# Second-half attention tiles: the minimum on GpSimd in integers, whole float32 probabilities, and the product with v on two column halves

## The chip, the core and the metric

The kernel runs on one core of a Trainium2 chip. Its five engines have queues of their own and meet by semaphores: TensorE (PE in the rows, with its weight loads as PEld), VectorE (DVE), ScalarE (ACT), GpSimd (POOL) and SyncE (SP, which issues DMAs). The metric is the device time of one execution in microseconds; lower is better.

## The reference, cut to what matters

Attention with a top-32 mask comes first, then a mixture of experts, then a gated MLP over all 2304 tokens (4 batches of 576 tokens, 8 heads of 64).

```python
scores = scale * np.matmul(q, k.transpose(0, 1, 3, 2))                  # 576 x 576 for each head
kth = np.partition(scores, -top_k, axis=-1)[..., -top_k:-top_k + 1]     # top_k = 32
attn = exp(where(scores >= kth, scores, -1e9) - max);  attn /= attn.sum(-1) + 1e-9
x = np.matmul(attn, v)                                                  # then reshaped to 2304 x 512
...                                                                     # routed experts, each row to one of 8
out = (silu(x @ w_gate) * (x @ w_val)) @ w_out                          # gated MLP, 512 -> 1536 -> 512
```

## The kernel before

Work is cut by pairs of heads: 16 pairs (4 batches with 4 each), and 9 tiles of 128 rows in a pair, 144 tiles in all. The first 9 pairs (81 tiles) are called `whole` in the code; they run alone, and the other 7 pairs (63 tiles) run while the experts and the gated MLP of the first two batches are woven between them. The page calls none of this by name, so the text calls them the first stage (13 to 336 us of the profile) and the second stage (336 to 812 us). After 858 us no attention is left: the experts and the MLP of the other two batches follow.

A tile goes through these steps. `head` makes the scores of 128 rows against 576 keys on TensorE (L226, bank `pS`) and ScalarE copies them to `sc` (L236). `rows_tile` finds the 32nd largest score of each row on VectorE: it takes the larger of the two halves of a row elementwise (L247, 288 wide) and the smaller (L265, or the pair L262 and L263), then runs the 8-at-a-time maximum and its replacement (L252, L267, L268), and the last maximum reads both halves, 576 wide. In the first stage the smaller half comes from GpSimd with the scores read as 32-bit integers: sum of both halves (`sm`, L262), minus the larger (L263); and the mask is made on TensorE (L277) and ScalarE (L278). In the second stage the smaller half is a VectorE minimum (L265), and VectorE also makes the masked probabilities `pp` from `sc`, the 32nd value and the exponentials `e` (L281).

`late` takes the probabilities on. In the first stage (`trans_whole`, `pv_whole`) `pp` is transposed as it is, in float32, 5 transposes for a tile (L321), copied to `pt` (L323), and multiplied with v, 5 float32 products of 64 columns (L331), then transposed back (L337). In the second stage GpSimd first splits `pp` into a high and a low part `pr` in the one-pass type float32r (L285 to L287), TensorE makes 9 transposes (L295) and 9 products with v, which is split as well (`vv`, L183 and L184; products L305), and a product with `fold` adds the two halves of 64 partitions (L312). A pair makes four products with v: two of 256 rows and two of 320. `prep` loads and transposes q and k of a pair; their copies into `nat` are made by GpSimd in the first stage and by ScalarE in the second (L163), and by ScalarE for the very first pair, which borrows the two `pr` buffers so that two of its four steps need not wait for the single `nat`.

The order on each engine comes from a scheduler at build time. It follows the order in which the code is written (one string for each stage says when transposes and products of earlier tiles come), with its own estimate of costs; the experts and the MLP are issued between tiles in proportion to the tiles that are done.

Of the kernel before, what the change touches and what calls it, by code (L numbers as in the profile page):

```python
# [32 lines left out]
class Kernel:  # L33
# [78 lines left out]

    def prep(self, R, b, h, whole):
        """Loads a pair of heads and puts what its tiles need into R; yields between steps."""
# [3 lines left out]

        def tile_of(nm):
            return (sb.tile([P, 2, 5, D], F32, name="vv", bufs=3) if nm == "v" and whole else  # L120
                    sb.tile([P, 2, 5, D], F32, name="raw", bufs=2))

        def load(nm, t, i, parts=(0, 1)):
# [19 lines left out]
        raws = {nm: tile_of(nm) for nm in ("k", "q")}  # L143
# [6 lines left out]
        for i in range(2):  # L150
            for nm, w in (("k", 2), ("q", 3)):
# [3 lines left out]
                if first and (i == 0) == (nm == "q"):  # L155
                    t = sb.tile([P, 2 * S], F32R, name="pr", bufs=2)[:, :15 * D].rearrange("p (c e) -> p c e", c=5)
                else:
                    t = sb.tile([P, 5, 3 * D], F32R, name="nat", bufs=1)
                o = t[:, :n, :w * D].rearrange("p c (t e) -> p c t e", t=w)
                src = raws[nm][:, i, :n, :]  # L160
                if first or (not whole):
                    for z in range(0, w, 2):
                        nc.scalar.activation(o[:, :, z, :], src, AF.Copy)  # L163
                elif w == 3:
                    nc.gpsimd.tensor_scalar(o[:, :, 0:3:2, :], src[:, :, None, :].to_broadcast([P, n, 2, D]),
                                            1.0, 1.0, op0=OP.mult, op1=OP.mult)
                else:
                    nc.gpsimd.tensor_scalar(o[:, :, 0, :], src, 1.0, 1.0, op0=OP.mult, op1=OP.mult)
# [70 lines left out]
    def rows_tile(self, R, i, c, Z, on_pe, sc):  # L239
        nc, ps, S = self.nc, self.ps, self.S  # L240
        sb, X = (self.at1, 1) if on_pe else (self.at, 0)
        W = S // 2
        scf = sc.rearrange("p a b -> p (a b)")
        rest = sb.tile([P, 2, W], F32, name="rest", bufs=3 if X else 2)
        hj, lo = rest[:, 0], rest[:, 1]
        hi = sb.tile([P, W], F32, name="hi", bufs=3) if X else hj
# [8 lines left out]
        pp = sb.tile([P, S], F32, name="pp", bufs=3 if X else 2)  # L255
# [15 lines left out]
        if on_pe:  # L271
            u = sb.tile([P, 2, W], F32R, name="e", bufs=3)
            nc.scalar.activation(u, sc, AF.Relu, bias=kth, scale=-1.0)
            pS = self.ps1.tile([P, 2, 512], F32, name="pM", bufs=1)
            self.scores(R, i, c, pS, stop=False)
            for x in range(2):
                nc.tensor.matmul(pS[:, x, :W], self.nidr, u[:, x, :], start=False, stop=True)  # L277
            nc.scalar.activation(pp.rearrange("p (a b) -> p a b", a=2), pS[:, :, :W], AF.Exp, bias=nb, scale=0.125,  # L278
                                 accum_out=Z)
        else:  # L280
            nc.vector.scalar_tensor_tensor(pp, scf, kth, e, op0=OP.is_ge, op1=OP.mult, accum_out=Z)  # L281
        if on_pe:
# [7 lines left out]
    def trans(self, pr, dests):  # L290
        nc = self.nc
        for a, z in ((0, 4), (4, 8), (8, 9)):
            p = self.pt_bank(F32R)
            for c in range(a, z):
                self.anchor = nc.tensor.transpose(p[:, c - a, :], pr[:, c * P:(c + 1) * P], self.idr)  # L295
            pf = p.bitcast(F32)
            for (T, do, so, n) in dests:
                nc.scalar.activation(T[:, a:z, do:do + n], pf[:, :z - a, so:so + n], AF.Copy)  # L298

    def pv(self, R, i, T, W, outs):  # L300
        nc, sb, D = self.nc, self.at, self.D
        vv = R["v"][i]
# [13 lines left out]
    def trans_whole(self, pp, dests):  # L316
        nc = self.nc
        for a, z, k in ((0, 4, P), (4, 5, 64)):
            p = self.pt_bank()
            for c in range(a, z):  # L320
                nc.tensor.transpose(p[:k, c - a, :], pp[:, c * P:c * P + k], self.idn)  # L321
            for (T, do, so, n) in dests:
                nc.scalar.activation(T[:k, a:z, do:do + n], p[:k, :z - a, so:so + n], AF.Copy)  # L323

    def pv_whole(self, R, i, T, W, outs):
        nc, sb, D = self.nc, self.at, self.D
        v = R["v"]
        po = self.pt_bank().rearrange("p a b -> p (a b)")
        for n in range(5):
            k = P if n < 4 else 64  # L330
            nc.tensor.matmul(po[:D, :W], v[:k, i, n, :], T[:k, n, :W], start=(n == 0), stop=(n == 4))  # L331
        oT = sb.tile([P, 320], F32, name="oT", bufs=1)[:D]
        nc.scalar.activation(oT[:, :W], po[:D, :W], AF.Copy)
        yield
        p = self.pt_bank()
        for j, (so, n, dst) in enumerate(outs):
            nc.tensor.transpose(p[:n, j, :D], oT[:, so:so + n], self.idn[:D, :D])  # L337
        for j, (so, n, dst) in enumerate(outs):
            nc.scalar.activation(dst, p[:n, j, :D], AF.Copy)

# [925 lines left out]
```

## Time and profile before

| what | value |
|---|---|
| median of 3 runs | 1313.6 us (1313.06 to 1316.07) |
| the profiled execution: span from first to last instruction | 1314.5 us |
| VectorE, TensorE, GpSimd busy in the first stage (323 us) | 315.2, 311.5, 223.5 us |
| the same in the second stage (476 us) | 445.5, 436.4, 321.5 us |
| the same from 858 us on (456 us) | 264.1, 434.5, 171.0 us |

The profiled execution's span is 0.9 us above the median of the runs, so one may stand for the other. Busy time is the time covered by an engine's records. Records of TensorE overlap: each one lasts from a matmul's start to its end, and the next starts before that end, so its busy time is more than the time that the work needs.

### The profile page before, as it was taken

What the parts mean: (1) busy time and instruction counts of PE and PEld (TensorE: products, weight loads), DVE (VectorE), ACT (ScalarE), POOL (GpSimd) and SP (SyncE); (2) the same over time, 40 slices, a digit from 0 to 9 for tenths busy, and PEclk for the clock granted to TensorE, in tenths of its full rate; (3) what the DMA queues carried; (4) which work ended last, traced back from release to release, by engine and by line L of the source; (5) the groups of instructions that cost most, each with busy time, mean ns of one, the idle gap of its engine ahead of it and who ended that gap; (6) DMA issues with size and microseconds to landing.
All of it is one profiled execution on the core that took longest, in us unless ns stands there. A gap on an engine that the chain in (4) does not pass through costs nothing.

```text
span 1314.5 us, 22493 instructions
## 1 busy us (share of the span) xinstructions
PE 1229.2 (94%) x7499; PEld 1076.6 (82%) x7500; DVE 1043.6 (79%) x2390; ACT 790.7 (60%) x1734; POOL 740.5 (56%) x888
## 2 busy tenths in 40 slices
PE   6899999999998998998998999899999999999995
PEld 5677777777787887887987789889998789898994
DVE  7999999999988889899999998217888638275570
ACT  5888887888855565665655545317677634343440
POOL 6866765766466676876787656413131335555550
PEclk9999999999998999997989999999999999999998
DMA  6411110101177787864556675469888644453520
GB/s 186 172 55 38 38 38 20 34 25 28 38 253 270 251 285 245 292 220 150 181 185 236 233 269 188 163 216 348 282 295 271 206 167 128 125 170 122 153 80 27
DMA packets 128577, 219.68 MB, mean 167 GB/s; under 512 B 20420, under 2 KB 86980, under 8 KB 122180
## 3 DMA queue, kind: packets, MB, share of 16 engines
q1 hardware_dynamic: 121428, 179.37, 41.6%
q0 software_dynamic: 7024, 38.78, 9.2%
q8 instruction: 62, 1.02, 0.3%
q14 instruction: 63, 0.52, 0.1%
HBM read 178.28 MB, written 41.95 MB: 168 GB/s over the span
## 4 chain that ended last, share of the span: by engine, by line
PE 36%; DVE 16%; DMA 5%; issue 3%; ACT 2%; POOL 2%; SPq 0%; DVEq 0%; ACTq 0%; POOLq 0%
PE m L1191 6%; PE m L1193 6%; PE m L1192 6%; PE m L1214 3%; PE m L1215 3%; PE m L1216 3%; DVE pp L281 3%; DVE tops L268 3%; DMA wraw<-in_moe_w_dram 2%; DVE rest L267 2%; DVE rest L247 2%; DVE rest L265 1%; DVE whl L664 1%; PE m L1124 1%; PE pT L295 1%
## 5 line engine op out<-in xcount | busy, mean ns | idle before, releaser
L268 DVE MAX8 tops<-rest 128x8 f32<-128x288 f32 (+1 forms) x432 | 227.2, 544 | 1.6
L1191 PE MATMUL m<-x2h,whl 128*128 128x384 f32 x576 | 198.0, 345 | 8.4 <-DVE th L1200 3.5
L1192 PE MATMUL m<-x2l,whl 128*128 128x384 f32 x576 | 196.7, 342 | 0.0
L1193 PE MATMUL m<-x2h,whl 128*128 128x384 f32 x576 | 196.4, 342 | 0.0
L1160 POOL TENSOR_TENSOR whl<-wfly,whl 128x1024 fp32r<-128x1024 f32 x54 | 129.8, 2404 | 109.0 <-ACT whl L1159 108.9
L267 DVE MATCH_REPLACE8 rest<-tops,rest 128x288 f32<-128x288 f32 x351 | 152.9, 437 | 0.0
L1159 ACT ACTIVATE whl<-wfly 128x1024 fp32r<-128x1024 f32 x69 | 73.2, 1061 | 97.9 <-PE m L1193 58.3
L236 ACT ACTIVATE sc<-pS 128x576 f32<-128x576 f32 x144 | 93.9, 652 | 54.5 <-DVE pp L281 38.6
L226 PE MATMUL pS<-kT,qT 128*128 128x288 f32 x512 | 108.8, 329 | 14.5 <-ACT sc L236 12.7
L1191 PEld LDWEIGHTS m<-x2h,whl 128*128 128x128 f32 x576 | 109.8, 191 | 10.7 <-DVE th L1200 4.4
L1192 PEld LDWEIGHTS m<-x2l,whl 128*128 128x128 f32 x576 | 110.2, 191 | 0.4
L1193 PEld LDWEIGHTS m<-x2h,whl 128*128 128x128 f32 x576 | 110.0, 191 | 0.5
L298 ACT ACTIVATE pt<-pT 128x512 fp32r<-128x512 f32 (+3 forms) x210 | 87.0, 464 | 35.1 <-PE pT L295 33.6
L1203 DVE TENSOR_TENSOR h2l<-th,h2h 128x384 fp32r<-128x384 f32 x36 | 85.9, 2386 | 21.5 <-ACT h2h L1202 21.5
L331 PE MATMUL pT<-pt,vv 128*64 128x256 f32 (+3 forms) x360 | 102.0, 415 | 0.8 <-ACT pt L323 0.8
L996 DVE TENSOR_TENSOR whl<-wraw,whl 128x1024 fp32r<-128x1024 f32 x64 | 80.2, 1266 | 27.7 <-ACT whl L995 23.6
L262 POOL TENSOR_TENSOR sm<-sc 128x288 int32<-128x288 int32 x81 | 73.5, 908 | 45.9 <-ACT sc L236 44.4
L226 PEld LDWEIGHTS pS<-kT,qT 128*128 128x128 f32 x512 | 79.5, 199 | 19.6 <-ACT sc L236 16.2
L1200 DVE SCALAR_TENSOR_TENSOR th<-th,m 128x384 f32<-128x384 f32 x72 | 39.0, 541 | 67.0 <-ACT th L1199 67.0
L995 ACT ACTIVATE whl<-wraw 128x1024 fp32r<-128x1024 f32 x64 | 67.5, 1060 | 38.0 <-DMA wraw<-in_moe_w_dram 23.3
L1214 PE MATMUL m<-whl,h2h 128*128 128x512 f32 x216 | 86.5, 404 | 2.4 <-ACT whl L642 1.7
L1215 PE MATMUL m<-whl,h2h 128*128 128x512 f32 x216 | 86.0, 398 | 0.0
(236 smaller groups left out, 3354.6 us busy)
## 6 DMA issues: line engine op xcount, KB each, us to landing
wfly<-w2s SPq DMA_DIRECT2D x69, 512.0 KB
whl<-in_moe_w_dram SPq DMA_DIRECT2D x32, 1024.0 KB
wraw<-in_moe_w_dram SPq DMA_DIRECT2D x64, 512.0 KB
whl<-w2s POOLq DMA_DIRECT2D x31, 1024.0 KB, 5.6
w2s<-h2h SPq DMA_DIRECT2D x8, 1024.0 KB
w2s<-whl SPq DMA_DIRECT2D x8, 1024.0 KB
io<-xa SPq DMA_DIRECT2D x18, 256.0 KB
out_dram<-io SPq DMA_DIRECT2D x18, 256.0 KB
```

Source lines behind the costliest of these rows:

```text
L226: m = self.nc.tensor.matmul(pS[:, x, :W], l, r[:, x * W:(x + 1) * W], start=(n == 0), stop=stop and n == len(ops) - 1)
L236: self.nc.scalar.activation(sc, pS[:, :, :W], AF.Copy, scale=BIG)
L267: nc.vector.match_replace(hj, h[:, (j - 1) * 8:j * 8], hi if j == 1 else hj, NEG)
L268: nc.vector.max(h[:, j * 8:(j + 1) * 8], hj if j < 3 else rest.rearrange("p a b -> p (a b)"))
L298: nc.scalar.activation(T[:, a:z, do:do + n], pf[:, :z - a, so:so + n], AF.Copy)
L331: nc.tensor.matmul(po[:D, :W], v[:k, i, n, :], T[:k, n, :W], start=(n == 0), stop=(n == 4))
L1160: self.fly_engine.tensor_tensor(lo, raw, hi.bitcast(F32), op=OP.subtract)
L1191: nc.tensor.matmul(pz, wh[:, z, k, :], xh[:, k, :], start=(k == 0), stop=False)
L1192: nc.tensor.matmul(pz, wh[:, z, k, :], xl[:, k, :], start=False, stop=False)
L1193: nc.tensor.matmul(pz, wl[:, z, k, :], xh[:, k, :], start=False, stop=(k == 3))
L1214: nc.tensor.matmul(po[t], hh[:, f, s], wh[:, k, :], start=(f == 0), stop=False)
L1215: nc.tensor.matmul(po[t], hh[:, f, s], wl[:, k, :], start=False, stop=False)
```

## The change

For the 63 tiles of the second stage: the smaller half is made by GpSimd in integers, as in the first stage; `pp` is not split, it is transposed in float32; v is not split; the copies of q and k into `nat` move from ScalarE to GpSimd. For all 144 tiles: the five products with v write the two halves of the 128 PSUM partitions in turn (products 0, 2, 4 to the lower 64, products 1 and 3 to the upper), and the product with `fold` adds them, where the first stage had a transpose back. The first pair no longer borrows `pr` buffers, which are gone: all four of its steps use the single `nat`. Buffers `hi`, `rest` and `pp` are three deep in both stages. All the rest (comments, an own tile `xt` for a copy that used `pp`) is the same work.

```diff
 prep:
-                if first and (i == 0) == (nm == "q"):
-                    t = sb.tile([P, 2 * S], F32R, name="pr", bufs=2)[:, :15 * D].rearrange("p (c e) -> p c e", c=5)
-                else:
-                    t = sb.tile([P, 5, 3 * D], F32R, name="nat", bufs=1)
+                t = sb.tile([P, 5, 3 * D], F32R, name="nat", bufs=1)
...
-                if first or (not whole):
+                if first:
                     for z in range(0, w, 2):
                         nc.scalar.activation(o[:, :, z, :], src, AF.Copy)
...
-        R["v"] = vv = []
-        for i in range(2):
-            t = sb.tile([P, 5, 2 * D], F32R, name="vv", bufs=3)
-            nc.gpsimd.tensor_scalar(t[:, :, :D], raw[:, i], 1.0, 1.0, op0=OP.mult, op1=OP.mult)
-            nc.gpsimd.tensor_tensor(t[:, :, D:], raw[:, i], t[:, :, :D].bitcast(F32), op=OP.subtract)
-            vv.append(t)
-            yield
 rows_tile:
-        if X:
-            sm = sb.tile([P, W], I32, name="sm", bufs=2)
-            sci = sc.bitcast(I32)
-            nc.gpsimd.tensor_tensor(sm, sci[:, 0, :], sci[:, 1, :], op=OP.add)
-            nc.gpsimd.tensor_tensor(lo.bitcast(I32), sm, hi.bitcast(I32), op=OP.subtract)
-        else:
-            nc.vector.tensor_tensor(lo, sc[:, 0, :], sc[:, 1, :], op=OP.min)
+        sm = sb.tile([P, W], I32, name="sm", bufs=2)
+        sci = sc.bitcast(I32)
+        nc.gpsimd.tensor_tensor(sm, sci[:, 0, :], sci[:, 1, :], op=OP.add)
+        nc.gpsimd.tensor_tensor(lo.bitcast(I32), sm, hi.bitcast(I32), op=OP.subtract)
...
-        pr = sb.tile([P, 2 * S], F32R, name="pr", bufs=2)
-        nc.gpsimd.tensor_scalar(pr[:, :S], pp, 1.0, 1.0, op0=OP.mult, op1=OP.mult)
-        nc.gpsimd.tensor_tensor(pr[:, S:S + 64], pp[:, 512:], pr[:, 512:S].bitcast(F32), op=OP.subtract)
-        nc.gpsimd.tensor_tensor(pr[:, S + 64:], pp[:, :512], pr[:, :512].bitcast(F32), op=OP.subtract)
-        return pr
 trans:
-        for a, z in ((0, 4), (4, 8), (8, 9)):
-            p = self.pt_bank(F32R)
+        for a, z, k in ((0, 4, P), (4, 5, 64)):
+            p = self.pt_bank()
             for c in range(a, z):
-                self.anchor = nc.tensor.transpose(p[:, c - a, :], pr[:, c * P:(c + 1) * P], self.idr)
+                self.anchor = nc.tensor.transpose(p[:k, c - a, :], pp[:, c * P:c * P + k], self.idn)
 pv:
-        for n in range(9):
-            self.anchor = nc.tensor.matmul(po[:, :W], vv[:, n if n < 5 else n - 5, :], T[:, n, :W], start=(n == 0),
-                                           stop=(n == 8))
+        for n in range(5):
+            k = P if n < 4 else 64
+            self.anchor = nc.tensor.matmul(po[(n % 2) * D:(n % 2 + 1) * D, :W], v[:k, i, n, :], T[:k, n, :W],
+                                           start=(n < 2), stop=(n >= 3))
...
-    def trans_whole(self, pp, dests):
-    def pv_whole(self, R, i, T, W, outs):
```

How the order on the engines moves is shown at three places of the second stage. On VectorE, behind the row update of the third expert: `sc` are the scores, `rest` and `hi` the halves, `tops` the list of maxima, `pp` the masked probabilities. Before:

```order
L247 TENSOR_TENSOR rest<-sc 128x288
L265 TENSOR_TENSOR rest<-sc 128x288
L252 MAX tops_67<-rest 128x8
L267 MATCH_REPLACE rest<-tops_67,rest 128x288
L281 SCALAR_TENSOR_TENSOR pp,z<-sc,tops_67,e 128x576
L268 MAX tops_67<-rest 128x8
L267 MATCH_REPLACE rest<-tops_67,rest 128x288
L268 MAX tops_67<-rest 128x8
```

The same place after the change (L230 is the old L247, L235 the old L252, L247 and L248 the old L267 and L268, L252 the old L281):

```order
L230 TENSOR_TENSOR hi<-sc 128x288
L235 MAX tops_67<-hi 128x8
L247 MATCH_REPLACE rest<-tops_67,hi 128x288
L248 MAX tops_67<-rest 128x8
L252 SCALAR_TENSOR_TENSOR pp,z<-sc,tops_67,e 128x576
L247 MATCH_REPLACE rest<-tops_67,rest 128x288
L248 MAX tops_67<-rest 128x8
```

The minimum between the maximum of halves and the first list is gone; nothing else of a tile leaves the engine. On GpSimd, around the scatter of the second expert's rows to DRAM (`xa<-io`) and the next gather (`io<-xa`), before:

```order
L1012 DMA xa_203<-io,ids_5335 1153x512
L285 TENSOR_SCALAR pr<-pp 128x576
L286 TENSOR_TENSOR pr<-pp,pr 128x64
L287 TENSOR_TENSOR pr<-pp,pr 128x512
L643 TENSOR_TENSOR h2h<-h2h 128x1024
L1005 DMA io<-xa_203,ids_5335 128x512
```

The same place after the change:

```order
L960 DMA xa_201<-io,ids_5307 1153x512
L244 TENSOR_TENSOR sm<-sc 128x288
L417 TENSOR_TENSOR x<-x,rt 64x64
L237 TENSOR_SCALAR nb<-tops_67 128x1
L245 TENSOR_TENSOR rest<-sm,hi 128x288
L244 TENSOR_TENSOR sm<-sc 128x288
L245 TENSOR_TENSOR rest<-sm,hi 128x288
L237 TENSOR_SCALAR nb<-tops_67 128x1
L953 DMA io<-xa_201,ids_5307 128x512
```

The three splits of `pp` are replaced by the integer pair, which now stands behind the scatter and ahead of the gather. On TensorE, around a product with v of 320 rows (`pt` and `vv`), before:

```order
L305 MATMUL pT<-pt,vv 128x320 x8
L295 MATMUL pT<-idr,pr 128x128 x4
L305 MATMUL pT<-pt,vv 128x320
L295 MATMUL pT<-idr,pr 128x128 x4
L1106 MATMUL m<-idn,th 128x128 x4
L226 MATMUL pS<-kT,qT 128x288 x4
L295 MATMUL pT<-idr,pr 128x128
L312 MATMUL pT<-fold,oT 128x64 x2
```

The same place after the change:

```order
L280 MATMUL pT<-pt,vv 64x320 x5
L269 MATMUL pT<-idn,pp 128x128 x4
L269 MATMUL pT<-idn,pp 64x128
L209 MATMUL pS<-kT,qT 128x288 x4
L1054 MATMUL m<-idn,th 128x128 x4
L287 MATMUL pT<-fold,oT 128x64 x2
```

Nine one-pass products become five float32 products of 64 columns, and nine transposes become five; the scores and the experts' work keep their places among them.

## Rows read from the trace of the kernel before

**Rows 1.** Stages: busy us (instructions) of PE, PEld, DVE, ACT, POOL; clock, DMA share, GB/s.

```profile
13.00:336.00 323.00, 311.51 (x2007) 240.12 (x2008) 315.21 (x968) 271.88 (x709) 223.47 (x353) 0.98 0.20 61
336.00:812.00 476.00, 436.41 (x2784) 393.42 (x2785) 445.52 (x1071) 279.36 (x667) 321.48 (x396) 0.95 0.67 224
858.00:1314.00 456.00, 434.47 (x2435) 399.72 (x2433) 264.07 (x302) 215.19 (x299) 170.95 (x88) 0.98 0.58 187
```

**Rows 2.** VectorE's groups, second stage: count, busy us, mean ns, idle before them, releaser.

```profile
L281 DVE SCALAR_TENSOR_TENSOR pp<-sc,tops,e 128x576 f32<-128x576 f32 x59 | 67.7, 1151 | 7.7 <-POOL pr L287 7.7
L247 DVE TENSOR_TENSOR rest<-sc 128x288 f32<-128x288 f32 x62 | 49.5, 798 | 16.6 <-ACT sc L236 16.6
L265 DVE TENSOR_TENSOR rest<-sc 128x288 f32<-128x288 f32 x62 | 45.3, 731 | 0.0
```

**Rows 3.** The chain that ended last, around 691 us: start, us, what.

```profile
691.75 3.45 DVE pp L281 x2
```

**Rows 4.** Timeline of the same stretch: start, us, engine, instruction.

```profile
691.21 2.40 POOL L643 TENSOR_TENSOR whl<-one,whl 128x1024 fp32r<-128x1024 f32 x1
691.75 3.44 DVE L281 SCALAR_TENSOR_TENSOR pp<-sc,tops,e 128x576 f32<-128x576 f32 x1
...
693.58 1.00 POOL L1203 TENSOR_TENSOR h2l<-th,h2h 128x384 fp32r<-128x384 f32 x1
...
698.93 0.80 DVE L281 SCALAR_TENSOR_TENSOR pp<-sc,tops,e 128x576 f32<-128x576 f32 x1
...
699.66 0.45 DVE L247 TENSOR_TENSOR rest<-sc 128x288 f32<-128x288 f32 x1
```

**Rows 5.** The maximum of halves in the first stage, VectorE's group.

```profile
L247 DVE TENSOR_TENSOR hi<-sc 128x288 f32<-128x288 f32 x81 | 50.0, 618 | 8.8 <-ACT sc L236 8.5
```

**Rows 6.** GpSimd's groups, second stage.

```profile
L287 POOL TENSOR_TENSOR pr<-pp,pr 128x512 fp32r<-128x512 f32 x59 | 80.0, 1356 | 0.0
L285 POOL TENSOR_SCALAR pr<-pp 128x576 fp32r<-128x576 f32 x59 | 44.4, 753 | 32.1 <-PE pT L295 17.0 <-DVE pp L281 13.9
L286 POOL TENSOR_TENSOR pr<-pp,pr 128x64 fp32r<-128x64 f32 x59 | 27.2, 462 | 3.5
...
L184 POOL TENSOR_TENSOR vv<-raw,vv 128x320 fp32r<-128x320 f32 x14 | 14.1, 1010 | 0.7
...
L1012 POOL DMA_INDIRECT xa<-io,ids x8 | 11.3, 1407 | 16.5 <-DVE io L1140 16.3 <-DMA w2s<-h2h 0.2
```

**Rows 7.** GpSimd's integer pair, first stage.

```profile
L262 POOL TENSOR_TENSOR sm<-sc 128x288 int32<-128x288 int32 x81 | 73.5, 908 | 45.9 <-ACT sc L236 44.4
L263 POOL TENSOR_TENSOR rest<-sm,hi 128x288 int32<-128x288 int32 x81 | 66.3, 819 | 22.8 <-DVE hi L247 15.0 <-DVE tops L268 5.1 <-DVE r_oh L540 0.7
```

**Rows 8.** TensorE's groups of transposes and products with v, whole execution (a float32 product shows twice).

```profile
L295 PE MATMUL pT<-idr,pr 128*128 128x128 f32 x567 | 73.6, 255 | 6.9 <-ACT kT L203 2.8 <-ACT oT L308 1.7 <-ACT pt L298 1.5
...
L321 PE MATMUL pT<-idn,pp 128*128 128x128 f32 x324 | 53.9, 289 | 0.0
...
L331 PE MATMUL pT<-pt,vv 128*64 128x320 f32 x144 | 42.6, 439 | 0.3 <-ACT pt L323 0.3
...
L305 PE MATMUL pT<-pt,vv 128*128 128x320 f32 x126 | 28.1, 357 | 2.8 <-ACT pt L298 2.8
...
L321 PE MATMUL pT<-idn,pp 128*64 128x128 f32 x81 | 23.2, 286 | 0.0
...
L312 PE MATMUL pT<-fold,oT 128*128 128x64 f32 x112 | 17.5, 281 | 0.0
...
L331 PE MATMUL pT<-pt,vv 64*64 64x320 f32 x36 | 13.5, 454 | 0.0
...
L337 PE MATMUL pT<-idn,oT 64*128 64x64 f32 x72 | 11.6, 241 | 0.0
```

**Rows 9.** Timeline of the first pair's steps on ScalarE and TensorE.

```profile
5.84 0.47 ACT L163 ACTIVATE pr<-raw 128x320 fp32r<-128x320 f32 x1 [1.48 <-DMA raw<-in_q_dram]
...
6.84 0.37 PE L209 MATMUL pR<-idr,nat 128*128 128x128 f32 x1 [1.16 <-ACT kT L203]
```

More of the change, by code (lines that the diff above doesn't have):

```diff
@@ L109, in late_constants, with prep @@
         self.w2s = self.dram.tile([self.NU, P, 3, WU], F32, name="w2s")
-    def prep(self, R, b, h, whole):
+    def prep(self, R, b, h):
         nc, sb, D, S = self.nc, self.at, self.D, self.S
         first = self.npair == 0
-        def tile_of(nm):
-            return (sb.tile([P, 2, 5, D], F32, name="vv", bufs=3) if nm == "v" and whole else
-                    sb.tile([P, 2, 5, D], F32, name="raw", bufs=2))
         def load(nm, t, i, parts=(0, 1)):
@@ L132, in load @@
             if nm == "v":
-                for r in range(2):
-                    eng.dma_start(t[r * 64:(r + 1) * 64, i, 4, :], tail)
+                eng.dma_start(t[:64, i, 4, :], tail)
             else:
@@ L142, in prep @@
         R.update(kT=kT, qT=qT, qt=qt)
-        raws = {nm: tile_of(nm) for nm in ("k", "q")}
+        raws = {nm: sb.tile([P, 2, 5, D], F32, name="raw", bufs=2) for nm in ("k", "q")}
         for nm in ("k", "q"):
@@ L239, in rows_tile @@
     def rows_tile(self, R, i, c, Z, on_pe, sc):
-        nc, ps, S = self.nc, self.ps, self.S
-        sb, X = (self.at1, 1) if on_pe else (self.at, 0)
+        nc, S = self.nc, self.S
+        sb = self.at1 if on_pe else self.at
         W = S // 2
         scf = sc.rearrange("p a b -> p (a b)")
-        rest = sb.tile([P, 2, W], F32, name="rest", bufs=3 if X else 2)
+        rest = sb.tile([P, 2, W], F32, name="rest", bufs=3)
         hj, lo = rest[:, 0], rest[:, 1]
-        hi = sb.tile([P, W], F32, name="hi", bufs=3) if X else hj
+        hi = sb.tile([P, W], F32, name="hi", bufs=3)
         nc.vector.tensor_tensor(hi, sc[:, 0, :], sc[:, 1, :], op=OP.max)
@@ L254, in rows_tile @@
         nc.gpsimd.tensor_scalar(nb, h[:, 0:1], -0.125 / BIG, 1.0, op0=OP.mult, op1=OP.mult)
-        pp = sb.tile([P, S], F32, name="pp", bufs=3 if X else 2)
+        pp = sb.tile([P, S], F32, name="pp", bufs=3)
         if not on_pe:
@@ L270, in rows_tile @@
             nc.gpsimd.tensor_tensor(self.FL[:, self.nlx - 9:self.nlx], tops[:, :, 23], tops[:, :, 31], op=OP.subtract)
[L271 to L280, printed above, removed]
+        if not on_pe:
@@ L290, in trans @@
-    def trans(self, pr, dests):
+        u = sb.tile([P, 2, W], F32R, name="e", bufs=3)
+        nc.scalar.activation(u, sc, AF.Relu, bias=kth, scale=-1.0)
+        pS = self.ps1.tile([P, 2, 512], F32, name="pM", bufs=1)
+        self.scores(R, i, c, pS, stop=False)
+        for x in range(2):
+            nc.tensor.matmul(pS[:, x, :W], self.nidr, u[:, x, :], start=False, stop=True)
+        nc.scalar.activation(pp.rearrange("p (a b) -> p a b", a=2), pS[:, :, :W], AF.Exp, bias=nb, scale=0.125,
+                             accum_out=Z)
@@ L314, in pv, with late @@
             nc.scalar.activation(dst, p[:n, j, :D], AF.Copy)
-    def trans_whole(self, pp, dests):
[L317 to L323, printed above, removed]
-    def pv_whole(self, R, i, T, W, outs):
[L326 to L339, printed above, removed]
     SEQ = [(0, 0), (0, 1), (0, 2), (0, 3), (0, 4), (1, 0), (1, 1), (1, 2), (1, 3)]
     DST = {0: (0, 0), 1: (0, 128), 2: (1, 0), 3: (1, 128), 5: (2, 64), 6: (2, 192), 7: (3, 0), 8: (3, 128)}
-    def late(self, R, j, n, pr, x, PT, whole):
-        trans, pv = (self.trans_whole, self.pv_whole) if whole else (self.trans, self.pv)
+    def late(self, R, j, n, pr, x, PT):
+        pv = self.pv
         if n in (0, 2, 4, 7):
-            PT[j, {0: 0, 2: 1, 4: 2, 7: 3}[n]] = (
-                self.at.tile([P, 5, 320], F32, name="pt", bufs=2) if whole else
-                self.at.tile([P, 9, 320], F32R, name="pt", bufs=2))
+            PT[j, {0: 0, 2: 1, 4: 2, 7: 3}[n]] = self.at.tile([P, 5, 320], F32, name="pt", bufs=2)
         if n == 4:
@@ L389, in start @@
             R[w] = {}
-            return self.prep(R[w], g * self.BG + b, 2 * j, whole(w))
+            return self.prep(R[w], g * self.BG + b, 2 * j)
         def late(w, n, pr):
             g, b, j = w
-            yield from self.late(R[w], w, n, pr, X[w], PT, whole(w))
+            yield from self.late(R[w], w, n, pr, X[w], PT)
             if n == 8:
@@ L478, in finish_pair @@
         nc.tensor.transpose(p2[:, 0, :64], x[:64, 4, :], self.idn[:64, :64])
-        xt = at.tile([P, S], F32, name="pp", bufs=2)
+        xt = at.tile([P, S], F32, name="xt", bufs=1)
         nc.scalar.activation(xt[:, :512], p.rearrange("p a b -> p (a b)"), AF.Copy)
```

14 lines of the change are left out of this document (6 added, 8 removed).

## The prediction, made before the changed kernel was run

> **What bounds the kernel now.** I read the busy time by stage first, to see which engine is full where the change acts. In the first stage VectorE covers 315.2 of 323 us (97.6%) and TensorE 311.5 (96.4%); in the second VectorE 445.5 of 476 (93.6%), TensorE 436.4 (91.7%), GpSimd 321.5 (67.5%), ScalarE 59%; from 858 us on TensorE has 95% and no attention is left [rows 1]. So the change can act on the first 858 us alone, and there two engines are nearly full at once: VectorE ends the wait, TensorE stands close behind.
>
> Next the groups of VectorE in the second stage. Three of its operations read two tensors: the masked product at L281 (1151 ns), the maximum of halves (798 ns) and the minimum (731 ns) [rows 2]. These means are not their own length. The chain of waits holds one piece of 3.45 us at L281 [rows 3], and the timeline shows why: it starts 0.5 us into a 2.40 us subtraction on GpSimd, a second one of 1.00 us follows, and it ends with that; the next L281, with less beside it, takes 0.80 us, and the maximum behind it 0.45 us [rows 4]. A VectorE operation on two tensors of SBUF waits out the GpSimd operation that it meets. "GPSIMD Engine Reference" of the Trainium skill (Key points) states the same: GpSimd shares its SBUF interfaces with VectorE, with contention where VectorE has two SBUF inputs; the trace agrees by the 3.44 us row.
>
> **The change, part by part.**
>
> *VectorE, second stage.* The minimum goes: 62 of the 63 lie in this stage, 45.3 us [rows 2]. The idle time ahead of L281, 7.7 us behind the GpSimd split `pr` [rows 2], goes as well, since `pp` is no longer read there and has three buffers. The splits that VectorE met also go, and the integer pair comes in their place. The maximum of halves has that pair beside it in the first stage and takes 618 ns [rows 5] against 798 here: 62 x 0.18 = 11 us. L281 can lose between nothing and 59 x (1.15 - 0.80) = 21 us; I take half, 10, as the maximum of halves loses 0.18 of the 0.35 by which it exceeds 0.45. VectorE then has 445.5 - 45.3 - 21 = 379 us, and of its 30.5 us idle 23 remain: alone it would end the stage after 402 us, 74 earlier.
>
> *GpSimd, second stage.* Out go the splits of `pp`, 80.0 + 44.4 + 27.2, and of v, at least 14.1: 166 us [rows 6]. In come 62 pairs of 0.908 + 0.819 us [rows 7], 107 us, and some 28 copies into `nat` of q and k, which I bound by the 753 ns of a 576-wide copy [rows 6] at 21 us. That leaves 284 us or less. It covers fewer us than now, so it isn't full; its lateness is a rival below. ScalarE loses one of three copies for each tile and those of `nat`, and was at 59%: worth nothing.
>
> *TensorE, transposes.* A tile's nine one-pass transposes cover 73.6/63 = 1.17 us; five float32 ones cover (53.9 + 23.2)/81 = 0.95 [rows 8]: 63 x 0.22 = 14 us less.
>
> *TensorE, product with v.* The first stage's 18 products of 320 rows take (42.6 + 13.5)/18 = 3.12 us each, the second stage's 14 take 28.1/14 = 2.01 [rows 8]. The 256 wide ones scale by width, so a pair (two of each) costs 3.6 times these: 11.2 us as float32, 7.2 as split. What the column halves do no row shows: no two products of 64 columns beside each other write different halves. The bounds: if they run one after the other, 11.2 us a pair; if a product overlaps the neighbour on the other half, then of ten passes (two for each product) the second pass of one runs with the first of the next, which makes six steps, 6.7 us. "TensorEngine Tiling (Array Packing)" (Key Properties) states that tiles operate independently and can load weights and multiply in parallel; by its "up to 2x" a pair would cost 5.6 us; no run here shows it yet. I take 6.7, because each half writes its own partitions and the weights come as separate 64-column loads; the other end is a rival. In the second stage, 7 pairs: -3.5 us, or +28. In the first, 9 pairs: -41 us, or 0. There the products with `fold` replace the transposes back: 17.5/56 = 0.31 against 11.6/72 = 0.16 us [rows 8], ten a pair, 90 x 0.15 = +13 us. So the first stage's TensorE work changes by -28 or +13 us.
>
> *What becomes of the freed time.* TensorE is what is late next. With 436.4 - 14 - 3.5 = 419 us of records it would end the stage after 419/0.964 = 435 us if it were as full as in the first stage [rows 1]: 41 us earlier. If its present 40 us of idle stayed, 459 us: 17 earlier. The idle follows VectorE's chain mostly, so it should shrink; I take 38 us. The mean granted clock is 0.95 there against 0.98 in the first stage [rows 1], that is, parts of it ran at 1.2 GHz instead of 2.4; denser work could only help, and I count nothing.
>
> *First stage.* VectorE has 97.6% and keeps every operation. Of its 7.8 us of idle I give 2 to a TensorE that is relieved of 28 us. The cover is VectorE itself: without the overlap the 13 us would push TensorE past 323 us of records, and I would count +4.
>
> *Start.* The second step of the first pair (ScalarE at 5.84 us) now waits until the first step's last transpose has read `nat` (6.84 + 0.37 us) [rows 9]: 1.4 us at most, and as its transposes waited for their bank anyway, 1 us.
>
> Sum: -38 - 2 + 1 = -39 us on the profiled 1314.5; the median of the runs lies 0.9 below that, 1313.6, so 1275 us.
>
> **Rivals.**
>
> *The halves run one after the other.* For: no row shows them together. TensorE then has 436.4 - 14 + 28 = 450 us, 467 at the first stage's share: -9; its records overlap, so the true need is lower and -20 is possible; -15 with +4 and +1 gives 1304 us.
>
> *The minimum arrives late.* VectorE takes its instructions in order, and the last maximum of a tile needs the GpSimd result. "GPSIMD Engine Reference" (Engine selection) sends two-input elementwise work to VectorE, as about twice slower on GpSimd; here the pair takes 1.73 us for 0.73. By that the change is wrong only if GpSimd's lateness reaches VectorE. Against: in the first stage GpSimd is 69% covered with the same pair and VectorE is idle for under 8 us [rows 1]. For: in the second stage the pair stands behind scatters that idle GpSimd 16.5 us [rows 6] and behind 16 subtractions of 2.4 us [rows 4], 55 us together. If half passes to VectorE, 27 of the 38 us are lost: 1303 us.
>
> *Slower: TensorE sets the stage with its idle as it is.* If the halves don't overlap and the waits around TensorE stay (ScalarE's copies, PSUM banks), the stage takes 450 + 40 = 490 us, +14; with +4 and +1 this gives 1332 us. It decides from a price of 7.2 + 14/7 = 9.2 us for a pair's products upwards.
>
> *It doesn't do what it says.* VectorE's time is freed but the experts' work woven between the tiles keeps the pace: 1313 us.
>
> **How the numbers follow.** Forecast 0.58 (its own range 1258 to 1292: between -17 and -56 us in the second stage, the low end half way from TensorE's to VectorE's limit), halves in turn 0.17, late minimum 0.13, slower 0.08, nothing 0.04. VectorE's own limit, 1240 us, is unlikely since TensorE stands before it; the range 1254 to 1306 leaves out some 0.06 below and 0.13 above. A measurement of this kernel tells 0.2% (2.6 us) from no change. Slower by more: 0.08 and a little of the other cases, 0.10; within: 0.05; faster: 0.85.
>
> **What the profile after would show.** VectorE's busy time in the second stage near 380 us, the mean of L281 (then L252) under 1.1 us, no idle time of VectorE on GpSimd's `rest`. TensorE's share of the second stage higher than 91.7%, near that of the first. A 320-row product near 1.9 us instead of 3.1. The first stage within 3 us of 323, the part behind the attention as long as now. The prediction is wrong if that product takes 3 us or more, if VectorE idles behind the integer pair, or if TensorE's idle stays though VectorE is freed.

## The result and the profile after

The changed kernel takes 1265.9 us (median of 4 runs, 1263.9 to 1270.2) against 1314.2 for the kernel before on the same chip (4 runs, 1313.1 to 1316.1): a ratio of 0.962, interval 0.960 to 0.965. The prediction said 1275. Sign and range hold; the gain is 48 us instead of 39, and two of its terms are off by more than that difference.

The view of the stages of the changed kernel, cut where the first tile, tile 81 and the last tile begin (busy us and instructions of PE, PEld, DVE, ACT, POOL; clock, DMA share, GB/s):

```profile
13.60:317.60 304.00, 293.62 (x2131) 238.90 (x2131) 303.81 (x962) 270.18 (x715) 221.23 (x359) 0.98 0.22 67
317.60:763.00 445.40, 420.97 (x2541) 348.81 (x2541) 408.70 (x1020) 236.66 (x559) 276.23 (x340) 0.97 0.71 237
763.00:1264.00 501.00, 475.18 (x2673) 434.11 (x2673) 279.19 (x339) 228.28 (x336) 182.92 (x106) 0.98 0.57 184
```

The kernel before, cut in the same way:

```profile
13.20:335.70 322.50, 311.01 (x2006) 239.80 (x2005) 314.72 (x966) 271.62 (x708) 223.27 (x353) 0.98 0.20 61
335.70:811.60 475.90, 436.31 (x2783) 393.13 (x2782) 445.42 (x1072) 279.58 (x668) 321.48 (x396) 0.95 0.67 224
811.60:1314.50 502.90, 476.02 (x2691) 439.02 (x2689) 279.70 (x342) 232.74 (x342) 191.39 (x117) 0.98 0.57 183
```

So the first stage gives 18.5 us, the second 30.5, the rest 1.9, and the start costs 0.4: 50.5 us of profiled span. The first stage, for which 2 us had been counted, brings over a third of it.

VectorE's groups of the changed kernel in the second stage (count, busy us, mean ns, idle before them):

```profile
L252 DVE SCALAR_TENSOR_TENSOR pp<-sc,tops,e 128x576 f32<-128x576 f32 x61 | 67.8, 1112 | 2.1 <-PE pT L269 2.1
...
L230 DVE TENSOR_TENSOR hi<-sc 128x288 f32<-128x288 f32 x62 | 49.6, 800 | 5.9 <-ACT sc L219 5.6
L248 DVE MAX8 tops<-rest 128x8 f32<-128x576 f32 x64 | 47.9, 750 | 4.0 <-POOL rest L245 2.3
```

The minimum is gone, but the maximum of halves takes 800 ns as before (798) and the masked product 1112 (1151) [rows 2]: neither became shorter as forecast, and VectorE is covered for 408.7 us, not 379. The last maximum waits only 2.3 us for the integer pair, which on GpSimd is this (same view and stage):

```profile
L245 POOL TENSOR_TENSOR rest<-sm,hi 128x288 int32<-128x288 int32 x63 | 58.0, 920 | 24.7 <-DVE hi L230 19.9 <-DVE tops L248 2.1 <-DMA io<-xa 1.1
L244 POOL TENSOR_TENSOR sm<-sc 128x288 int32<-128x288 int32 x62 | 56.3, 907 | 37.5 <-ACT sc L219 36.8
```

The pair waits for VectorE and ScalarE, not they for it. TensorE's groups of the changed kernel, whole execution:

```profile
L269 PE MATMUL pT<-idn,pp 128*128 128x128 f32 x576 | 93.4, 282 | 1.0 <-ACT kT L186 0.5 <-ACT kT L197 0.4
L280 PE MATMUL pT<-pt,vv 128*64 128x320 f32 x256 | 41.5, 445 | 3.5 <-DVE L L441 2.9 <-ACT pt L271 0.5
L269 PE MATMUL pT<-idn,pp 128*64 128x128 f32 x144 | 40.3, 280 | 0.0
...
L280 PE MATMUL pT<-pt,vv 64*64 64x320 f32 x64 | 24.0, 455 | 0.0
```

There are 32 products with v of 320 rows (a float32 product shows as two records): (41.5 + 24.0)/32 = 2.05 us each, against 3.12 in the first stage before [rows 8]. Neighbours on different halves do run together; e5 below changes their order alone.

### The profile page after: what moved, and what is told of

It reads as the page before. It is cut to its first block, busy times and chain, and to the rows that moved or that the text cites. A ratio compares the mean times of both kernels' runs of the same rounds, so it can differ in the third digit from the quotient of the medians.

```text
span 1264.0 us, 21890 instructions
## 1 busy us (share of the span) xinstructions
PE 1195.6 (95%) x7365; PEld 1026.5 (81%) x7366; DVE 994.6 (79%) x2327; ACT 741.2 (59%) x1622; POOL 684.8 (54%) x825
## 5 line engine op out<-in xcount | busy, mean ns | idle before, releaser
L248 DVE MAX8 tops<-rest 128x8 f32<-128x288 f32 (+1 forms) x432 | 231.2, 546 | 5.7 <-POOL rest L245 2.3
L244 POOL TENSOR_TENSOR sm<-sc 128x288 int32<-128x288 int32 x144 | 124.5, 865 | 61.9 <-ACT sc L219 58.8
L245 POOL TENSOR_TENSOR rest<-sm,hi 128x288 int32<-128x288 int32 x144 | 125.0, 868 | 53.5 <-DVE hi L230 43.7
L271 ACT ACTIVATE pt<-pT 128x512 f32<-128x512 f32 (+2 forms) x320 | 115.9, 404 | 37.0 <-PE pT L269 35.3
L247 DVE MATCH_REPLACE8 rest<-tops,rest 128x288 f32<-128x288 f32 x288 | 125.9, 438 | 0.0
L280 PE MATMUL pT<-pt,vv 128*64 128x256 f32 (+3 forms) x640 | 121.1, 424 | 4.9 <-DVE L L441 2.9
L269 PE MATMUL pT<-idn,pp 128*128 128x128 f32 (+1 forms) x720 | 119.3, 281 | 1.0 <-ACT kT L186 0.5
L269 PEld LDWEIGHTS pT<-idn,pp 128*128 128x128 f32 (+1 forms) x720 | 79.7, 137 | 39.0 <-issue 26.9
L230 DVE TENSOR_TENSOR hi<-sc 128x288 f32<-128x288 f32 x144 | 96.5, 670 | 11.1 <-ACT sc L219 10.8
```

The source lines that it names most:

```text
L247: nc.vector.match_replace(hj, h[:, (j - 1) * 8:j * 8], hi if j == 1 else hj, NEG)
L248: nc.vector.max(h[:, j * 8:(j + 1) * 8], hj if j < 3 else rest.rearrange("p a b -> p (a b)"))
L269: self.anchor = nc.tensor.transpose(p[:k, c - a, :], pp[:, c * P:c * P + k], self.idn)
L280: self.anchor = nc.tensor.matmul(po[(n % 2) * D:(n % 2 + 1) * D, :W], v[:k, i, n, :], T[:k, n, :W], start=(n < 2), stop=(n >= 3))
```

## The experiments

The edits are to the changed kernel, in two cases to the kernel before. The table takes the profiled executions apart as above. How much of the woven experts' work is done when the last tile begins differs between the kernels, so the column "behind", from tile 81 (the first of the second stage) to the end, is what is compared. Both columns come from one execution of each kernel; the ratio comes from all its runs. The clock is TensorE's granted clock in the second stage.

| kernel | first stage | second | behind | clock | ratio to before, interval |
|---|---|---|---|---|---|
| before | 322.5 | 475.9 | 978.8 | 0.95 | 1 |
| changed | 304.0 | 445.4 | 946.4 | 0.97 | 0.962, 0.960 to 0.965 |
| e1_one_half | 318.7 | 453.0 | 958.4 | 1.00 | 0.986, 0.982 to 0.991 |
| e2_first_stage_halves | 304.9 | 475.1 | 976.5 | 0.95 | 0.983, 0.979 to 0.986 |
| e3_min_on_vector | 304.4 | 423.5 | 953.3 | 0.97 | 0.964, 0.959 to 0.968 |
| e4_min_only | 323.0 | 505.7 | 1000.7 | 0.93 | 1.016, 1.012 to 1.020 |
| e5_halves_in_turn | 339.8 | 444.7 | 950.8 | 0.99 | 0.992, 0.989 to 0.994 |
| e6_max_first | 304.2 | 408.4 | 939.8 | 0.97 | 0.956, 0.951 to 0.961 |
| e7_whole_only | 318.3 | 456.9 | 963.7 | 0.98 | 0.983, 0.979 to 0.986 |
| e8_one_more_max | 334.3 | 439.2 | 966.6 | 0.95 | 0.997, 0.994 to 0.999 |
| e9_change_again | 303.5 | 451.2 | 953.8 | 0.98 | 0.961, 0.958 to 0.963 |
| e10_max_first_again | 304.4 | 408.1 | 937.6 | 0.98 | 0.955, 0.953 to 0.957 |

e9 is the changed kernel once more and e10 is e6 once more. The stages of e9:

```profile
13.60:317.10 303.50, 293.29 (x2131) 238.73 (x2130) 302.50 (x961) 270.25 (x715) 223.85 (x359) 0.99 0.22 67
317.10:768.30 451.20, 420.42 (x2541) 347.03 (x2541) 410.36 (x1020) 236.45 (x559) 279.72 (x340) 0.98 0.70 233
768.30:1270.90 502.60, 476.62 (x2674) 435.69 (x2673) 279.39 (x339) 228.70 (x336) 183.19 (x106) 0.98 0.56 183
```

They show how far a row can be trusted: the first stage comes out within 0.5 us of the first time, but "behind" is 953.8 against 946.4 us for the same kernel. A difference of some 7 us in "behind" between two rows can therefore be chance, and the sums of such differences below are rough.

**e1_one_half**: all products on the lower 64 partitions, with the transposes back in place of `fold`.

```diff
-            self.anchor = nc.tensor.matmul(po[(n % 2) * D:(n % 2 + 1) * D, :W], v[:k, i, n, :], T[:k, n, :W],
-                                           start=(n < 2), stop=(n >= 3))
+            self.anchor = nc.tensor.matmul(po[:D, :W], v[:k, i, n, :], T[:k, n, :W], start=(n == 0), stop=(n == 4))
...
-            nc.tensor.matmul(p[:n, j, :D], oT[:, so:so + n], self.fold, start=True, stop=True)
+            nc.tensor.transpose(p[:n, j, :D], oT[:, so:so + n], self.idn[:D, :D])
```

> The changed kernel, but all five products with v write the lower 64 partitions and a transpose back replaces the product with fold, in both stages. Theory (the halves overlap, and the first stage's 18.5 us came from that): the 320-row product rises from 2.05 to about 3.1 us, the first stage goes back from 304 to about 322 us, the second stage loses 5 to 20 us; about 1265.9 + 18 + 12 = 1296 us. Rival (the first stage gained by buffers or by another order of instructions): the first stage stays near 304 us and the time stays below 1280 us.

1296.1 us. The column halves with their fold are worth 318.7 - 304.0 = 14.7 us in the first stage and 12.0 behind it, the latter a rough figure: the execution behind this row was the fastest of four, 3.7 us below their median.

**e3_min_on_vector**: in the second stage the minimum goes back to VectorE, all else stays.

```diff
+        if on_pe:
             sm = sb.tile([P, W], I32, name="sm", bufs=2)
...
+        else:
+            nc.vector.tensor_tensor(lo, sc[:, 0, :], sc[:, 1, :], op=OP.min)
```

> The changed kernel, but the minimum of the second stage is VectorE's again; splits stay away. Theory (VectorE still bounds the second stage together with TensorE, so its minimum was worth most of the stage's 30.5 us): 62 minima of 0.45 to 0.75 us come back, the integer pair leaves GpSimd; second stage about 20 to 30 us longer, about 1288 us. Rival (the gain of the second stage came from the splits of pp that are gone, and VectorE has room): less than 8 us longer, below 1274 us.

1269.5 us (1265.6 to 1273.1, against 1263.9 to 1270.2): the two can't be told apart, so the move of the minimum, which the title names first, is worth little or nothing here. The 20 to 30 us expected of it are refuted. VectorE's groups of this kernel in the second stage show why:

```profile
L255 DVE SCALAR_TENSOR_TENSOR pp<-sc,tops,e 128x576 f32<-128x576 f32 x60 | 53.3, 889 | 1.2 <-PE pT L272 1.2
...
L230 DVE TENSOR_TENSOR hi<-sc 128x288 f32<-128x288 f32 x62 | 39.4, 635 | 6.3 <-ACT sc L219 6.3
L248 DVE TENSOR_TENSOR rest<-sc 128x288 f32<-128x288 f32 x62 | 36.0, 581 | 0.0
```

Without the pair on GpSimd the maximum of halves takes 635 ns instead of 800 and the masked product 889 instead of 1112; the minimum itself costs 581. A tile saves 0.58 us by the move and gives back 0.17 + 0.22: 36 us less 24, so 12 us of VectorE's time in all. "Behind" differs by 6.9 us, which is no more than e9 differs from the changed kernel.

**e5_halves_in_turn**: the order of the five products alone, so that neighbours write the same half but once.

```diff
-        for n in range(5):
+        for n in (0, 2, 4, 1, 3):
```

> The changed kernel with the five products with v in the order 0, 2, 4, 1, 3: three on the lower half, then two on the upper. Same work and buffers. Theory (neighbours on different halves overlap, pass by pass): only one change of halves is left, nine steps instead of six, a 320-row product takes about 2.8 us instead of 2.05; first stage 8 to 14 us longer, about 1283 us in all. Rival (products of 64 columns with a fold are faster whatever their order): no change, 1266 us.

1305.1 us. A row of TensorE's timeline in the first stage of this kernel (start, us; it joins the ten passes of the five products):

```profile
207.56 3.19 PE L280 MATMUL pT<-pt,vv 128*64 128x320 f32 x10
```

Such rows of the changed kernel, and of e1 with all products on one half, at the same width:

```profile
53.69 1.98 PE L280 MATMUL pT<-pt,vv 128*64 128x320 f32 x10
```

```profile
399.05 3.05 PE L280 MATMUL pT<-pt,vv 128*64 128x320 f32 x10
```

The same ten passes with the same destinations take 3.19 us instead of 1.98 when the halves don't alternate, no less than on one half alone. So the expectation missed in its size (2.8 us, 1283 us in all): the picture of single passes that overlap with their neighbour comes near the 1.98 (six steps of ten, 1.83 of 3.05), but the one change of halves that is left should have saved a tenth, and nothing of that shows. The first stage loses 35.8 us by it, more than twice what e1 loses; that `fold` costs more than the transposes back is part of it, and what the whole of the difference is made of stays open. Behind it this kernel loses only 4.4 us, at a clock of 0.99.

**e2_first_stage_halves**: the kernel before, with only the column halves and `fold` put into `pv_whole`.

```diff
-            nc.tensor.matmul(po[:D, :W], v[:k, i, n, :], T[:k, n, :W], start=(n == 0), stop=(n == 4))
+            nc.tensor.matmul(po[(n % 2) * D:(n % 2 + 1) * D, :W], v[:k, i, n, :], T[:k, n, :W], start=(n < 2),
+                             stop=(n >= 3))
...
-            nc.tensor.transpose(p[:n, j, :D], oT[:, so:so + n], self.idn[:D, :D])
+            nc.tensor.matmul(p[:n, j, :D], oT[:, so:so + n], self.fold, start=True, stop=True)
```

> The kernel before, with nothing changed but the first stage's products with v: two column halves in turn and the product with fold. Theory (TensorE set the pace of the first stage, though VectorE was covered for 97.6% of it): the first stage falls from 322.5 us to about 305, the rest stays; about 1297 us, ratio 0.987. Rival (the shorter first stage of the changed kernel came from buffers, loads or order): first stage within 4 us of 322.5, ratio 0.997 to 1.003.

1294.5 us. This part alone shortens the first stage by 17.6 of the 18.5 us. Its row in the view of stages, first stage:

```profile
13.30:318.20 304.90, 293.82 (x2130) 238.47 (x2129) 304.76 (x965) 272.96 (x720) 220.98 (x356) 0.99 0.22 66
```

VectorE does the same operations as before and is covered for 304.8 us instead of 315: at 97.6% it was not full. Theory and time agree here (about 305 and 1297 expected). Its maximum of halves in that stage is a little shorter than the 618 ns of [rows 5]:

```profile
L247 DVE TENSOR_TENSOR hi<-sc 128x288 f32<-128x288 f32 x80 | 46.5, 582 | 0.1
```

**e4_min_only**: the kernel before with only the integer pair in the second stage; the splits stay, `hi` has one buffer there and the sum is made in place.

```diff
-        if X:
-            sm = sb.tile([P, W], I32, name="sm", bufs=2)
...
-        else:
-            nc.vector.tensor_tensor(lo, sc[:, 0, :], sc[:, 1, :], op=OP.min)
+        sm = sb.tile([P, W], I32, name="sm", bufs=2) if X else lo.bitcast(I32)
```

> The kernel before, with the second stage's minimum as the integer pair on GpSimd and nothing else of the change (the splits of pp stay on GpSimd; one buffer for the maximum, the sum written in place). By the step of the prediction (VectorE ends the second stage, its minimum is worth up to 45 us): 20 us faster or more, ratio below 0.985. Theory after the first runs (the minimum's place is worth little, and GpSimd, now asked for 107 us more on top of 321 in 476 us, is late): no gain or slower, ratio 1.00 to 1.03, with GpSimd at 85% or more of the second stage and VectorE idle behind its result.

1338.3 us: 1.6% slower than before, where the step of the prediction wanted 20 us less. Its row of the second stage in the view of stages:

```profile
336.10:841.80 505.70, 448.50 (x2798) 402.78 (x2798) 448.38 (x1011) 278.26 (x665) 430.93 (x521) 0.93 0.63 213
```

VectorE lost 62 minima and is covered for 448 us, 3 us more than before. Its groups there:

```profile
L278 DVE SCALAR_TENSOR_TENSOR pp<-sc,tops,e 128x576 f32<-128x576 f32 x59 | 81.5, 1384 | 23.5 <-POOL pr L284 23.3
L247 DVE TENSOR_TENSOR hi<-sc 128x288 f32<-128x288 f32 x62 | 60.2, 972 | 15.8 <-ACT sc L236 12.5 <-POOL rest L262 2.5 <-POOL vv L184 0.6
```

And its waits in the same stretch (us in total, times, longest):

```profile
DVE pp L278 <- POOL pr L284: 23.3, 14, 3.9
DVE hi L247 <- ACT sc L236: 12.5, 5, 4.2
DVE tops L265 <- POOL rest L262: 5.6, 5, 1.8
DVE hi L247 <- POOL rest L262: 2.5, 3, 1.3
```

With the splits and the pair both on GpSimd (431 of 506 us) VectorE's two-input operations grow to 1384 and 972 ns and it waits 31 us for GpSimd. "GPSIMD Engine Reference" of the Trainium skill (Engine selection) would keep such work on VectorE; here that is borne out, and in the changed kernel, where GpSimd has room (276 of 445 us), the move gains little or nothing rather than losing. The single `hi` buffer, which this kernel alone has, shows as the 2.5 us of the last row; what its sum in place costs can't be told apart.

**e7_whole_only**: the edits of e1 and e3 together, so that of the change the whole probabilities and v, the copies into `nat` and the buffers remain.

> The changed kernel without the column halves (all products to the lower 64 partitions, transposes back) and with the second stage's minimum on VectorE: what is left is that probabilities and v are whole, and the copies of q and k on GpSimd. Theory (parts add up: of the 32 us behind the first stage 12 come from the halves, some 7 or less from the minimum): the first stage is back at about 319 us, the stretch behind it gains about 13 us on the kernel before; ratio 0.985 to 0.992. Rival (whole products cost TensorE more than the transposes save, 28 us against 14, and without the halves nothing is gained): ratio 0.998 to 1.01.

1294.8 us. The ratio, 0.983, lies just below the 0.985 to 0.992 of the theory. Behind the first stage what is left brings 978.8 - 963.7 = 15.1 us, though TensorE's products there are now undivided float32 ones. Which part of it does so (the splits that GpSimd no longer makes, four transposes fewer, the copies into `nat`, the buffers) was not tried apart. The first stage, in which none of this acts on the products, is 4.2 us shorter.

e7 and e1 differ only by the minimum's place, as e3 and the changed kernel do. VectorE's groups in the second stage, e7:

```profile
L255 DVE SCALAR_TENSOR_TENSOR pp<-sc,tops,e 128x576 f32<-128x576 f32 x60 | 59.8, 996 | 17.1 <-PE pT L272 17.0
L230 DVE TENSOR_TENSOR hi<-sc 128x288 f32<-128x288 f32 x62 | 39.6, 638 | 10.9 <-ACT sc L219 10.8
L248 DVE TENSOR_TENSOR rest<-sc 128x288 f32<-128x288 f32 x63 | 34.5, 548 | 0.0
```

And e1:

```profile
L252 DVE SCALAR_TENSOR_TENSOR pp<-sc,tops,e 128x576 f32<-128x576 f32 x61 | 62.0, 1017 | 12.5 <-PE pT L269 12.5
L230 DVE TENSOR_TENSOR hi<-sc 128x288 f32<-128x288 f32 x62 | 46.8, 756 | 10.3 <-ACT sc L219 9.0 <-issue 0.8
```

Here a tile saves 0.55 us and gives back 0.12 + 0.02: the longer maximum comes back in both pairs of kernels, the longer masked product in one only. The whole gains nothing by it (ratio 0.983 in e7, 0.986 in e1); TensorE is covered for 441 of 457 us in e7's second stage and 435 of 453 in e1's.

**e6_max_first**: GpSimd's pair made in another order, first score minus maximum, then plus the other score.

```diff
-        nc.gpsimd.tensor_tensor(sm, sci[:, 0, :], sci[:, 1, :], op=OP.add)
-        nc.gpsimd.tensor_tensor(lo.bitcast(I32), sm, hi.bitcast(I32), op=OP.subtract)
+        nc.gpsimd.tensor_tensor(sm, sci[:, 0, :], hi.bitcast(I32), op=OP.subtract)
+        nc.gpsimd.tensor_tensor(lo.bitcast(I32), sm, sci[:, 1, :], op=OP.add)
```

> The changed kernel with the integer pair in another order: first half of the scores minus the maximum, then plus the second half; the same result. Both GpSimd operations then wait for the maximum, so the sum no longer starts with it when the scores arrive. Theory (the maximum of halves is long, 574 ns in the first and 800 ns in the second stage against 450 alone, because it meets the GpSimd sum of the same scores): its mean falls to about 480 and 620 ns, 81 x 0.09 + 62 x 0.18 = 18 us less of VectorE's time, 10 to 18 us shorter, about 1252 us. Rival (the contention only moves to the masked product, or the minimum comes too late for the last maximum): 1266 us or longer, with idle time of VectorE behind the GpSimd result.

1257.5 us, the fastest so far. The first operation of the pair no longer starts on the same scores at the same moment as the maximum of halves, but behind it. Its groups on VectorE in the second stage:

```profile
L252 DVE SCALAR_TENSOR_TENSOR pp<-sc,tops,e 128x576 f32<-128x576 f32 x60 | 66.3, 1106 | 0.5 <-PE pT L269 0.3
...
L248 DVE MAX8 tops<-rest 128x8 f32<-128x576 f32 x63 | 47.2, 749 | 5.0 <-POOL rest L245 3.7
L230 DVE TENSOR_TENSOR hi<-sc 128x288 f32<-128x288 f32 x62 | 40.8, 658 | 5.0 <-ACT sc L219 5.0
```

The maximum of halves takes 658 ns, nearly what it takes with no pair at all (635): 62 x 0.14 = 9 us, less 1.4 us more waiting for the pair; "behind" is 6.6 us shorter. The masked product keeps its 1106 ns. The gain is 8 us, not the 10 to 18 expected: the first stage gives nothing, though the maximum of halves is shorter there too. The changed kernel's row and this kernel's, first stage:

```profile
L230 DVE TENSOR_TENSOR hi<-sc 128x288 f32<-128x288 f32 x81 | 46.5, 574 | 0.2 <-ACT sc L219 0.2
```

```profile
L230 DVE TENSOR_TENSOR hi<-sc 128x288 f32<-128x288 f32 x81 | 42.1, 520 | 1.8 <-ACT sc L219 1.8
```

That is 4.4 us less for VectorE, and the stage takes 304.2 us as before (304.0).

**e8_one_more_max**: one spare maximum over `hi` for each of the 144 tiles, its result unused.

```diff
+        nc.vector.max(sb.tile([P, 8], F32, name="spare", bufs=2), hi)
```

> The changed kernel with one more 8-fold maximum of 0.44 us on VectorE in every tile, into a tile that nobody reads. If VectorE sets the pace of a stage in full, the first grows by 81 x 0.44 = 36 us and the second by 63 x 0.44 = 28 us. Theory: the changed kernel's first stage is VectorE's (covered 304 of 304 us), +30 to +36; the second is shared with TensorE, +5 to +15; about 1306 us. Rival (TensorE sets the first stage as well): first stage +15 or less.

1313.0 us. VectorE's timeline in the first stage shows what the spare one takes:

```profile
101.28 0.45 DVE L235 MAX8 tops<-hi 128x8 f32<-128x288 f32 x1
101.66 0.44 DVE L236 MAX8 spare<-hi 128x8 f32<-128x288 f32 x1
102.01 0.07 DVE L248 MATCH_VALUE_LOAD rest<-tops,rest 128x8 f32 x1
```

Its record lasts 0.44 us, but the next instruction starts 0.35 us after it. For 81 tiles that is 28 us and the first stage grows by 30.3; for the other 63 it is 22 us and "behind" grows by 20.3, not the 5 to 15 expected (this execution's clock there is 0.95, the changed kernel's 0.97). So after the change what is added to VectorE comes on the time nearly in full. The reverse doesn't follow: in e6's first stage 4.4 us taken from VectorE brought nothing.

**e9_change_again and e10_max_first_again**: the changed kernel and e6, in five rounds on one chip.

> The changed kernel as it is, on the same chip as the next one, so that the two can be compared: ratio 0.960 to 0.965.

> The integer pair with the maximum first, once more. If the shorter contention with the maximum of halves is real, it is 5 to 9 us (0.4 to 0.7%) below the changed kernel beside it; if the first measurement was noise, the two ratios are equal within 0.2%.

1264.9 us (ratio 0.961, interval 0.958 to 0.963) and 1257.2 us (0.955, interval 0.953 to 0.957). The intervals don't meet: the other order is a version that beats both kernels, 0.6% below the changed one.

## Why the prediction was right in sum, and where its steps failed

- **The halves overlap: right.** It said 3.12 x 6/10 = 1.87 us for a 320-row product, and 2.05 were measured. "TensorEngine Tiling (Array Packing)" of the Trainium skill (Key Properties) has tiles multiply independently; 2.05 us bears it out, but the 3.19 us of e5 show that it takes more than two column halves: the neighbours in the queue must differ. The rival "the halves run one after the other" falls, except as e5, and so does "it doesn't do what it says" (1313 us).
- **TensorE's work: right in the second stage, but as a sum; too much in the first.** Records of 421.0 us there, forecast 419. Of its terms the product with v had the wrong sign: the groups of the second stage's 28 products add up to 55.3 us after and 49.3 before, 6 us more where 3.5 less were forecast. In the first stage 311.0 became 293.6, -17 instead of -28.
- **First stage, "VectorE has 97.6%", gain 2 us: mis-sized, 18.5 measured.** TensorE set the pace there: e2 changes nothing but TensorE's products and ScalarE's copy and gives 17.6. The covered share misled, since VectorE's records overlap (0.44 us long, the next 0.35 us later in e8): a small wait between two of them needn't show as idle time. Of the 10 us less cover, 3 are the maximum of halves (618 ns in [rows 5], 582 in e2); that the rest were such waits is argued, not shown.
- **VectorE, second stage, "the minimum goes, 45.3 us" and 21 us of shorter operations: this step failed.** The idle time of 7.7 us behind the splits did go. But the integer pair took the place of the splits as what VectorE's two-input operations meet, and they stayed at 800 and 1112 ns. VectorE had 408.7 us, not 379: 21 of the 30 us are this step, the rest is not taken apart. The forecast took over the 618 ns of the first stage [rows 5], where the pair is most of GpSimd's work (73.5 + 66.3 of 223.5 us, [rows 7] and [rows 1]). In the second stage GpSimd's other work, the experts' above all, lengthens the maximum to 635 ns without any pair (e3), and the pair comes on top.
- **What the freed time becomes: 38 us, 32.4 measured (30.5 in the second stage, 1.9 in the rest), and from other parts than thought.** Added one at a time to the kernel before, behind the first stage: whole probabilities and v with their buffers and copies 15.1 (before to e7), minimum on GpSimd 5.3 (e7 to e1), halves 12.0 (e1 to changed). In the other order, halves 10.4 (e7 to e3) and minimum 6.9 (e3 to changed). By e9's 7 us neither figure for the minimum is clear of noise, and by the ratios of all runs it is worth nothing without the halves (0.983 in e7, 0.986 in e1) and at most 0.2% with them (0.964 in e3, 0.962 in the changed kernel), with intervals that overlap both times. The minimum alone, with the splits still there, costs 21.8 us in e4's form (one `hi` buffer, the sum in place). The gain that the forecast gave to the minimum fits the splits that left GpSimd: with them gone and no pair (e3), VectorE's maximum, minimum and masked product take 635, 581 and 889 ns against 798, 731 and 1151. That the splits alone, without the rest of e7's edits, bring it is not shown.
- **The number: right in part by luck.** On the profiled span 16.5 us more in the first stage make up for 6 us less behind it, and the second stage came near its 38 us although VectorE was not freed as forecast. TensorE, which was to be late next there, was not alone: e8's 22 us on VectorE cost 20.3. The working also slips at the edges of its range: with its other terms -56 and -17 give 1257 and 1296, not 1258 and 1292.
- **"The minimum arrives late": rejected** as the forecast had it: 2.3 us of VectorE's idle time are put down to `rest`. What the pair costs is not lateness but the length of what runs beside it; lateness shows in e4, where GpSimd is 85% covered. **"Slower"** didn't come; its condition was a pair of heads at 9.2 us or more, and that pair's products now take 2 x 2.05 + 2 x 1.81 = 7.7 us (1.81 from the 256-row groups in the same way).
- **Start +1, rest unchanged, GpSimd under 284 us:** 0.4, -1.9 and 276.

Open: the 4 us of the first stage in e1 and e7, where the products are as before (buffers of `hi`, `rest` and `pp`, loads and order are what differ there, not tried apart); and TensorE's clock in the second stage. It is 1.00 in e1 and 0.99 in e5, where TensorE has 435 us and more of records, and 0.97 in the changed kernel with 421 and longer gaps. Part of what the halves free there, and of why e5 loses so little there, may lie in that; no run separates it.

## What to carry to other kernels

Before crediting an operation moved from VectorE to GpSimd, count what it lengthens: each VectorE operation with two SBUF inputs that meets it, measured here as 0.39 us a tile back for 0.58 saved in one pair of kernels and 0.14 for 0.55 in the other, and try making the GpSimd operation wait for the VectorE one that reads the same data. A covered share of 97% doesn't say which of two nearly full engines sets the pace; one spare instruction for each step, and its slope, tells more, though it prices time added and not time saved. Where products are narrower than the array, alternate their column halves instruction by instruction.

## What the hardware showed unexpectedly

An elementwise VectorE operation can spend most of its record waiting for GpSimd, and the other way round. VectorE's timeline of the changed kernel, second stage:

```profile
499.62 2.71 DVE L230 TENSOR_TENSOR hi<-sc 128x288 f32<-128x288 f32 x1
...
507.00 0.46 DVE L230 TENSOR_TENSOR hi<-sc 128x288 f32<-128x288 f32 x1
```

GpSimd's timeline of the same stretch:

```profile
499.39 2.36 POOL L591 TENSOR_TENSOR h2h<-h2h 128x1024 fp32r<-128x1024 f32 x1
501.72 0.21 POOL L250 TENSOR_TENSOR FL<-tops 128x9 f32<-128x9 f32 x1
501.89 1.08 POOL L244 TENSOR_TENSOR sm<-sc 128x288 int32<-128x288 int32 x1
...
507.05 1.07 POOL L244 TENSOR_TENSOR sm<-sc 128x288 int32<-128x288 int32 x1 [2.92 <-ACT sc L219]
```

The maximum that begins 0.2 us into a 2.36 us subtraction takes 2.71 us, and ends 0.4 us, its own length, after the small operation behind that one. The next begins 0.05 us ahead of the pair's sum and takes 0.46 us; there it is the sum that is longer, 1.07 us where the median of all 144 sums is 0.80. So the one that begins first is let through, and the whole trace bears it out for the maximum: of the changed kernel's 144, the 15 that begin ahead of the GpSimd operation that they meet take 0.43 to 0.46 us, the 30 that meet none take 0.40 to 0.46, and the 99 that begin while one is running take up to 3.03, 0.77 in the mean. In e6, whose pair begins only when the maximum has ended, those 99 are 63. And ten float32 passes of 64 columns, 320 wide, took 1.98 us with the halves in alternation and 3.19 in turn: the order of instructions alone decided whether the array's two halves worked at once.
